# Another order for the first steps of a pooled-attention and maxout kernel: one kv tile summed by TensorE, two others added on GpSimd

## The chip, the cores and the metric

The kernel runs on one core of a Trainium2 chip. A core has five engines that run their own queues of instructions: PE (TensorE, matmuls), DVE (VectorE), ACT (ScalarE), POOL (GpSimd) and SP (SyncE, which here only issues DMAs). The metric is the device time of one execution in microseconds (us); lower is better. Times of the kernel before: 1977.1, 1976.53 and 1977.3 us in three runs, median 1977.1.

## The reference

For each of four batches, 12288 queries of 128 channels attend to 768 keys. The keys are also the values; they come from a 384 x 32 map that is averaged over 4 x 4 windows and multiplied by `w_sr`. The attended rows go through three matrices at once, of which the elementwise maximum is taken, and one output matrix:

```python
kv_pool = kv.reshape(B, H // 4, 4, W // 4, 4, C).mean(axis=(2, 4))
k = v = kv_pool.reshape(B, -1, C) @ w_sr
s = (q @ k.transpose(0, 2, 1)) / np.sqrt(C)
a = np.exp(s - s.max(-1, keepdims=True))
a /= a.sum(-1, keepdims=True) + 1e-09
x = (a @ v).reshape(B * N, C)
h = np.maximum(np.maximum(x @ w1, x @ w2), x @ w3)      # d_ff = 768
out = h @ w_out
```

## The kernel before

The 49152 queries form 96 groups of 512 (four tiles of 128). Values that enter a matmul are split in two float16 parts, high and low, and every product is three matmuls (high by high, high by low, low by high). The maximum over three matrices is computed as `max(0, x(w2-w1), x(w3-w1))`, with `x w1 w_out` added at the end through a matrix `w1o` that is prepared once.

The program is written as a list of short tokens. `START` (lines 169 to 197) is the first part, `STEADY` the repeated middle, `END` the last. `run` (line 1187) executes the tokens in order, and an `InOrder` wrapper (line 98) keeps every engine's instructions in the order in which the tokens issue them, so a token's place sets its place in every queue that it uses. A `!` behind a token changes the engine: for `add`, `fold`, `qc`, `m`, `c`, `l`, `C`, `L` and the weight steps it swaps DVE with POOL or with ACT.

For a group, `S` makes the scores of one tile (six matmuls of 384 columns), `m` the negated row maximum on DVE and the bias `nb` from it, `e` the exponential on ACT, `c` and `l` the float16 parts (`ahl`; ACT and POOL as a rule), after which SP transposes `ahl` into `aT`. `X` multiplies by the values: tile by tile in group 0, later in two halves of a group. `xh`, `xl` split the result; `H` makes six matmuls for one of six column blocks of the hidden layer, `R` and `M` the maximum, `C` and `L` the split `hh`, `hl`; `O` multiplies by `w_out`. `z` is a matmul on constants whose result nobody reads (line 870).

In the first part the keys of batch 0 are made and six weight halves plus two of `w_out` are unpacked. The kv map of a batch is 12 tiles of 512 KB, numbered strip (0 to 2) and row in the window (0 to 3): `kv.s.i` loads one, `add.s.i.n` adds tile n to tile i (128 x 1024 float32), `fold.s.i.n` adds the second half of each window to its first half, and `gat.s.i` sums what is left by matmuls with the identity: eight of 128 columns for a raw tile, four for a folded one. `gd` copies the sums out, `gj` multiplies them by `w_sr`, `gp` and `gb` take the peaks, `gt`, `tops` and `sized` make one power of two out of them, `gh` and `gl` write the keys' two halves; the first `S` needs all of these. `qc` multiplies half a query block by a row of scales, `qp` takes its peak, `qt` turns a group of it by four matmuls with a scaled identity (`sr_e`), `qu` and `qv` split that. The weights go through `wd` (load), `wm` (scale), `ws` (shift), `wt` (column sums on PE), `wl` and `wn` (low bits and sign), `wr` (minus `w1`), `wh` and `wo` (the split). `wl`, `wn` on DVE read two tensors in SBUF.

Of the twelve tiles the kernel before adds `0.1` to `0.0`, `0.3` to `0.2` and their sums on DVE, adds `2.1` and `2.3` to `2.0` there and folds it, and gathers strip 1's four tiles and `2.2` raw. GpSimd has nothing to do there.

Of the kernel before, what the change touches and what calls it, by code (L numbers as in the profile page):

```python
# [21 lines left out]
def kernel(  # L22
# [32 lines left out]
    B, N, C = q.shape  # L55
    _, HH, WW, _ = kv.shape
    R = 4
# [3 lines left out]
    P = 128  # L61
    NKT = NK // P
    NFT = DF // P
    G = 512
# [21 lines left out]
    qp = ctx.enter_context(tc.tile_pool(name="qp", bufs=3))  # L86
# [50 lines left out]
    def spread(out, t, n, start, stop):  # L137
# [21 lines left out]
    wo = [const.tile([P, NFT // 2, 2, C], F16, name=f"wo{h}") for h in range(2)]  # L159
# [7 lines left out]
    HB_ = 5  # L167
    TURNED = 2
    START = (
# [27 lines left out]
    )  # L197
    STEADY = (
# [71 lines left out]
    tops = {}  # L270
# [956 lines left out]
```

## Time and profile before

| | |
|---|---|
| median of three runs | 1977.1 us |
| span of the profiled execution, first to last instruction | 1975.0 us |
| own time of the profiled execution | not listed apart from its span |
| PE busy | 1961.6 us (99%) |
| DVE, ACT, POOL busy | 1449.1, 1494.1, 1306.8 us |
| chain that ended last | PE 97%, DMA 1%, ACT 1% |
| granted TensorE clock | 1.000 over the span (its upper level, 2.4 GHz) |

The median lies 2.1 us above the span. The span holds from the first instruction to the last, so a stretch in which PE has nothing to do lengthens it one for one where PE is busy everywhere behind it. Busy matmuls overlap: a record of 379 ns for 512 columns is issued every 216 ns, so the duration of a row of matmuls is read from one row's start to the next.

### The profile page before, as it was taken

How to read it: one execution, taken by the hardware profiler on the slowest of the kernel's cores; microseconds unless marked ns; L12 is line 12 of the kernel's file. 1: busy time of each engine (PE TensorE's matmuls, PEld its weight loads, DVE VectorE, ACT ScalarE, POOL GpSimd, SP SyncE). 2: the span in 40 equal slices, each digit the busy share in tenths (PEclk: the TensorE clock that was granted, in tenths of full speed). 3: DMA queues.
4: the chain of work that ended last, by engine and by line, in shares of the span. 5: the costliest groups of instructions: out<-in, count | busy, mean ns of one | idle time of the engine just before them, and what ended most of it. 6: DMA issues, size and time to landing. Idle time of an engine off the chain costs nothing.

```text
span 1975.0 us, 29499 instructions
## 1 busy us (share of the span) xinstructions
PE 1961.6 (99%) x9826; PEld 960.4 (49%) x9826; DVE 1449.1 (73%) x2518; ACT 1494.1 (76%) x2628; POOL 1306.8 (66%) x963
## 2 busy tenths in 40 slices
PE   8999999999999999999999999999999999999999
PEld 6444444444444444444444444444444444444444
DVE  7877777777767777777767777777766776766677
ACT  5777777777777777777777777777777777777775
POOL 3576666666667667766676666776676666666663
PEclk9999999999999999999999999999999999999999
DMA  8678777667678778766668777866676666766663
GB/s 272 124 163 164 156 150 144 136 133 145 127 148 167 154 145 164 143 124 142 136 126 169 155 147 157 168 125 128 137 143 138 129 127 125 148 121 125 133 129 80
DMA packets 842696, 283.97 MB, mean 144 GB/s; under 512 B 816048, under 2 KB 817200, under 8 KB 842544
## 3 DMA queue, kind: packets, MB, share of 16 engines
q1 hardware_dynamic: 842256, 281.43, 70.2%
q8 instruction: 77, 1.26, 0.3%
q10 hardware_dynamic: 288, 0.66, 0.1%
q14 instruction: 75, 0.61, 0.1%
HBM read 53.54 MB, written 25.17 MB: 40 GB/s over the span
## 4 chain that ended last, share of the span: by engine, by line
PE 97%; DMA 1%; ACT 1%; POOL 0%; DVE 0%; issue 0%; SPq 0%; POOLq 0%; ACTq 0%
PE ps_h L106 37%; PE ps_o L106 22%; PE ps_x L106 19%; PE ps_s L106 19%; DMA kv_piece<-in_kv_dram 1%; POOL ahl L106 0%; DMA kv_piece<-in_moe_w_out_dram 0%; DMA aT<-ahl 0%; ACT a L106 0%; DVE mx L106 0%; POOL hl L106 0%; DVE w_e L106 0%; ACT ahl L106 0%; ACT w_e L106 0%; ACT h L106 0%
## 5 line engine op out<-in xcount | busy, mean ns | idle before, releaser
L106 POOL TENSOR_TENSOR hl<-h,hh 128x512 f16<-128x512 f32 x469 | 560.8, 1201 | 494.5 <-ACT hh L106 490.6
L106 POOL TENSOR_TENSOR ahl<-a,ahl 128x768 f16<-128x768 f32 x380 | 631.0, 1680 | 104.1 <-ACT ahl L106 79.2
L106 DVE SCALAR_TENSOR_TENSOR h<-ps_h,h 128x512 f32<-128x512 f32 x576 | 396.8, 689 | 365.8 <-PE ps_h L106 209.0
L106 ACT ACTIVATE h<-ps_h 128x512 f32<-128x512 f32 x576 | 343.1, 596 | 274.7 <-PE ps_h L106 264.0
L106 PE MATMUL ps_h<-xh,d_hi 128*128 128x512 f16 x1152 | 436.4, 379 | 0.5 <-ACT h L106 0.2
L106 PE MATMUL ps_h<-xl,d_hi 128*128 128x512 f16 x1152 | 436.4, 379 | 0.0
L106 PE MATMUL ps_h<-xh,d_lo 128*128 128x512 f16 x1152 | 436.4, 379 | 0.0
L106 DVE TENSOR_REDUCE mx<-ps_s 128x1 f32<-128x768 f32 x384 | 365.4, 952 | 51.8 <-PE ps_s L106 51.5
L106 ACT ACTIVATE a<-ps_s,nb,q_sc 128x768 f32<-128x768 f32 x384 | 379.5, 988 | 12.7 <-DVE nb L106 9.0
L106 PE MATMUL ps_s<-k_hi,qT 128*128 128x384 f16 x1536 | 374.7, 326 | 2.1 <-ACT a L106 1.9
L106 PE MATMUL ps_x<-aT,v_hi 128*128 128x512 f16 (+1 forms) x1188 | 366.2, 373 | 0.1
L106 ACT CAST hh<-h 128x512 f16<-128x512 f32 x573 | 333.2, 613 | 42.4 <-DVE h L106 42.4
L106 PEld LDWEIGHTS <-d_hi 128*128 128x128 f16 x2308 | 225.8, 98 | 256.5
L106 PE MATMUL ps_o<-hh,wo 128*128 128x512 f16 x1140 | 339.1, 379 | 0.0
L106 PEld LDWEIGHTS <-qT 128*128 128x128 f16 x2304 | 225.2, 98 | 191.2 <-issue 4.2
L106 ACT CAST ahl<-a 128x768 f16<-128x768 f32 x379 | 309.5, 829 | 7.4 <-DMA aT<-ahl 1.5
L106 PEld LDWEIGHTS <-wo 128*128 128x128 f16 x1710 | 167.3, 98 | 191.7 <-DVE o_planes L106 0.2
L106 PE MATMUL ps_s<-k_lo,qT 128*128 128x384 f16 x768 | 250.3, 326 | 0.0
L106 PE MATMUL ps_x<-aT,v_lo 128*128 128x512 f16 (+1 forms) x594 | 220.1, 373 | 0.0
L106 PE MATMUL ps_o<-hl,wo 128*128 128x512 f16 x570 | 216.0, 379 | 0.0
L106 PEld LDWEIGHTS <-v_hi 128*128 128x128 f16 x1188 | 115.3, 98 | 134.6 <-issue 0.2
L106 PEld LDWEIGHTS <-d_lo 128*128 128x128 f16 x1154 | 112.9, 98 | 122.6 <-issue 3.3
(159 smaller groups left out, 1433.7 us busy)
## 6 DMA issues: line engine op xcount, KB each, us to landing
q_sb<-in_q_dram SPq DMA_DIRECT2D x48, 512.0 KB, 4.4
out_dram<-o_sb SPq DMA_DIRECT2D x95, 256.0 KB, 2.0
kv_piece<-in_kv_dram SPq DMA_DIRECT2D x46, 512.0 KB, 4.5
aT<-ahl SPq DMA_TRANSPOSE x384, 4.0
kv_piece<-in_moe_w_dram SPq DMA_DIRECT2D x6, 384.0 KB, 10.0
o_turned<-o_planes SPq DMA_TRANSPOSE x95, 3.4
qT<-q_hl SPq DMA_TRANSPOSE x94, 3.2
kv_piece<-in_moe_w_out_dram SPq DMA_DIRECT2D x2, 384.0 KB, 4.6
```

What stands on the lines that cost most here:

```text
L106: return lambda **kw: tc.keep_in_program_order(op(**kw))
```

## The change

Only the table `START` changes; the functions, the middle and the end stay, and so does the number of every kind of compute token, with these exceptions. `add.0.2.3` and `gat.1.2` go; `gat.0.3`, `add.1.0.2!` (on GpSimd) and `fold.1.0.2` (on DVE) come. So tile `0.3`, the first loaded, is gathered raw, and strip 1's tiles 0 and 2 are added by GpSimd and folded. The gathers are 48 matmuls in place of 52. The query block is the third load: behind `0.3` on ACT's queue and `1.1` on SP's; strip 2 comes last, its tile 2 in two halves. Eleven `z` stay eleven: one of them stands ahead of the first `S` before, six now. Several weight steps, biases and splits change engine: `qc` twice and `wr` twice from DVE to GpSimd, `wn` twice the other way, `m` twice and `L` three times to GpSimd, `C` three times and `c` twice to DVE, `gd.3` from DVE to ACT. The last token of the new table leaves the same counts of `S`, `X`, `H` and `O` done as before.

```diff
     START = (
-        "qd sr si z ka qc! kv.1.3 gat.1.3 kv.0.2 qc! kv.2.2.0 gat.2.2.0 kv.0.1 qp",
-        "kv.2.2.1 kv.0.0 add.0.0.1 gat.2.2.1 kv.1.1 kv.2.1 add.0.2.3 gat.1.1 kv.2.0 qt add.0.0.2 add.2.0.1 kv.1.0 gat.0.0",
...
+        "z sr z kv.1.1 qd z kv.0.1 qc! si kv.0.0 gat.1.1 qc! kv.0.2 kv.1.0 kv.1.2",
+        "kv.1.3 add.0.0.1 gat.0.3 add.1.0.2! add.0.0.2 ka qp z kv.2.0 gat.0.0 qt qu gp.0 fold.1.0.2 qv",
...
```

GpSimd's queue from its first step on the data, before (`w_s` is a sign, `nb` a bias of `m`, `ahl` the low half of a score tile):

```order
L106 TENSOR_TENSOR w_e_290<-w_e_290,w_s_317 128x384
L106 TENSOR_SCALAR nb_366<-mx_364,q_sc_322 128x1
L106 TENSOR_TENSOR w_e_351<-w_e_351,w_s_375 128x384
L106 TENSOR_SCALAR nb_398<-mx_396,q_sc_322 128x1
L106 TENSOR_TENSOR ahl_409<-a_402,ahl_409 128x768
L106 TENSOR_TENSOR ahl_426<-a_424,ahl_426 128x768
L106 TENSOR_TENSOR ahl_438<-a_429,ahl_438 128x768
```

The same queue now (`kv_piece_189` and `_191` are tiles 1.0 and 1.2, `q_sb_323` the second query block, `ahl_394` the first score tile):

```order
L106 TENSOR_TENSOR kv_piece_189<-kv_piece_189,kv_piece_191 128x1024
L106 TENSOR_TENSOR w_e_284<-w_e_284,w_s_309 128x384
L106 TENSOR_TENSOR w_e_300<-w_e_300,w_s_359 128x384
L106 TENSOR_TENSOR q_sb_323<-q_sb_323,col_row_107 128x512
L106 TENSOR_SCALAR nb_388<-mx_386,q_sc_348 128x1
L106 TENSOR_TENSOR ahl_394<-a_382,ahl_394 128x768
L106 TENSOR_TENSOR q_sb_323<-q_sb_323,col_row_107 128x512
L106 TENSOR_TENSOR ahl_421<-a_416,ahl_421 128x768
L106 TENSOR_TENSOR ahl_445<-a_425,ahl_445 128x768
L106 TENSOR_SCALAR nb_468<-mx_466,q_sc_348 128x1
L106 TENSOR_TENSOR ahl_478<-a_453,ahl_478 128x768
L106 TENSOR_TENSOR w_e_375<-w_e_375,w_e_408 128x384
```

An addition of 1024 columns stands first, and two scalings of queries stand among the low halves.

DVE's queue around the query peak and the scaled identity `sr_e`, before (`kv_piece_197` is tile 0.0, `_178` tile 0.2, `_217` tile 2.0):

```order
L106 TENSOR_REDUCE q_row_190<-q_sb_150 128x1
L106 TENSOR_SCALAR q_row_190<-q_row_190 128x1
L106 TENSOR_SCALAR q_up_192<-q_row_190 128x1
L106 RECIPROCAL q_up_192<-q_up_192 128x1
L106 TENSOR_TENSOR kv_piece_197<-kv_piece_197,kv_piece_188 128x1024
L106 TENSOR_TENSOR kv_piece_178<-kv_piece_178,kv_piece_140 128x1024
L106 TENSOR_SCALAR sr_e_220<-ident_103,q_up_192 128x128
L106 TENSOR_TENSOR kv_piece_197<-kv_piece_197,kv_piece_178 128x1024
L106 TENSOR_TENSOR kv_piece_217<-kv_piece_217,kv_piece_206 128x1024
```

The same stretch now (`kv_piece_175` is tile 0.0, `_189` tile 1.0, `_215` tile 2.0):

```order
L106 TENSOR_TENSOR kv_piece_175<-kv_piece_175,kv_piece_166 128x1024
L106 TENSOR_TENSOR kv_piece_175<-kv_piece_175,kv_piece_187 128x1024
L106 TENSOR_REDUCE q_row_207<-q_sb_162 128x1
L106 TENSOR_SCALAR q_row_207<-q_row_207 128x1
L106 TENSOR_SCALAR q_up_209<-q_row_207 128x1
L106 RECIPROCAL q_up_209<-q_up_209 128x1
L106 TENSOR_SCALAR sr_e_226<-ident_103,q_up_209 128x128
L106 TENSOR_REDUCE pool_max_131<-ps_s_196 128x1
L106 TENSOR_TENSOR kv_piece_189<-kv_piece_189 128x2x256
L106 TENSOR_TENSOR qT_232<-ps_h_225,qT_232 128x4x128
L106 TENSOR_TENSOR kv_piece_215<-kv_piece_215,kv_piece_237 128x1024
```

The strip's additions moved ahead of the query peak, and the fold of strip 1's sum stands between `sr_e` and the addition of strip 2.

## Rows read from the trace of the kernel before

**Rows 1.** The page, busy time of each engine, and the chain's shares.
```profile
PE 1961.6 (99%) x9826; PEld 960.4 (49%) x9826; DVE 1449.1 (73%) x2518; ACT 1494.1 (76%) x2628; POOL 1306.8 (66%) x963
...
PE 97%; DMA 1%; ACT 1%; POOL 0%; DVE 0%; issue 0%; SPq 0%; POOLq 0%; ACTq 0%
```

**Rows 2.** Busy time by stretch: length, engines, granted clock, DMA share, GB/s.
```profile
26.60:60.00 33.40, 29.84 (x203) 16.90 (x203) 31.60 (x63) 29.57 (x55) 19.20 (x17) 1.00 0.76 157
60.00:100.00 40.00, 39.87 (x205) 20.03 (x204) 33.56 (x54) 27.42 (x50) 24.18 (x22) 1.00 0.62 118
```

**Rows 3.** PE in order of time: start, us, instruction, count, idle before.
```profile
14.19 2.05 PE L106 MATMUL ps_s<-ident,kv_piece 128*128 128x128 f32 x16 [0.32 <-DMA kv_piece<-in_kv_dram]
16.07 1.06 PE L106 MATMUL ps_h<-sr_e,q_sb 128*128 128x128 f32 x8
16.97 3.74 PE L106 MATMUL ps_s<-ident,kv_piece 128*128 128x128 f32 x32
...
26.65 0.48 PE L106 MATMUL ps_s<-k_hi,qT 128*128 128x384 f16 x2
...
39.24 2.11 PE L106 MATMUL ps_x<-ones 128*128 128x512 f16 x5
...
55.81 0.38 PE L106 MATMUL ps_x<-aT,v_hi 128*128 128x512 f16 x1
```

**Rows 4.** The chain of waits in order of time: start, us, what.
```profile
89.70 1.29 PE ps_h L106 x6
91.00 1.95 PE ps_s L106 x12
```

**Rows 5.** DVE in order of time, while the kv tiles land.
```profile
7.74 1.22 DVE L106 TENSOR_REDUCE q_row<-q_sb 128x1 f32<-128x1024 f32 x1
...
9.37 0.16 DVE L106 RECIPROCAL q_up<-q_up 128x1 f32<-128x1 f32 x1
12.89 2.36 DVE L106 TENSOR_TENSOR kv_piece<-kv_piece 128x1024 f32<-128x1024 f32 x2 [3.35 <-DMA kv_piece<-in_kv_dram]
```

**Rows 6.** ACT in order of time, ahead of the keys' high half.
```profile
23.71 1.06 ACT L106 ACTIVATE q_abs<-q_sb 128x1024 f16<-128x1024 f32 x1 [0.22 <-DVE q_sb L106]
...
25.21 0.82 ACT L106 ACTIVATE k_hi<-ps_s,k_up 128x256 f16<-128x256 f32 x2
```

**Rows 7.** By tile, whole trace: count, duration ns min/median/max, first and last start.
```profile
L106 POOL TENSOR_TENSOR ahl<-a,ahl x380: 1632/1643/2162, 32.6 to 1941.3; 128x768 f16<-128x768 f32 x190
L106 DVE SCALAR_TENSOR_TENSOR w_e<-kv_piece,w_e x12: 542/549/1221, 27.4 to 63.3; 128x384 int32<-128x384 int32 x12
L106 DVE TENSOR_SCALAR w_e<-w_e x8: 347/354/547, 24.6 to 45.2; 128x384 int32<-128x384 int32 x8
L106 POOL TENSOR_TENSOR w_e<-w_e,w_s x4: 992/1001/1003, 25.8 to 54.3; 128x384 f32<-128x384 f32 x4
L106 DVE SCALAR_TENSOR_TENSOR d_lo<-w_e,d_up,d_hi x4: 612/614/617, 46.4 to 59.1; 128x384 f16<-128x384 f32 x4
L106 DVE SCALAR_TENSOR_TENSOR q_hl<-q_sb,q_up,q_hl x94: 735/743/752, 29.4 to 1912.5; 128x512 f16<-128x512 f32 x94
L106 POOL TENSOR_SCALAR nb<-mx,q_sc x8: 267/561/1078, 29.2 to 99.6; 128x1 f32<-128x1 f32 x8
L106 POOL TENSOR_TENSOR q_sb<-q_sb,col_row x90: 1262/1272/1283, 76.1 to 1847.3; 128x512 f32<-128x512 f32 x90
```

**Rows 8.** POOL and DVE in order of time, at two places where both work.
```profile
50.08 1.64 POOL L106 TENSOR_TENSOR ahl<-a,ahl 128x768 f16<-128x768 f32 x1 [0.90 <-ACT ahl L106]
...
50.91 1.22 DVE L106 SCALAR_TENSOR_TENSOR w_e<-kv_piece,w_e 128x384 int32<-128x384 int32 x1
...
29.15 1.08 POOL L106 TENSOR_SCALAR nb<-mx,q_sc 128x1 f32<-128x1 f32 x1 [2.31 <-DVE mx L106]
...
32.61 1.64 POOL L106 TENSOR_TENSOR ahl<-a,ahl 128x768 f16<-128x768 f32 x1 [0.77 <-ACT ahl L106]
```

**Rows 9.** DMA issues: size, median us from issue to landing.
```profile
aT<-ahl SPq DMA_TRANSPOSE x12, 3.9
```

48 rows, old and new, of the table START are left out of this document.

## The prediction

> **What bounds the kernel.** I read the page's totals and its chain first: PE is busy for 1961.6 us of the 1975.0 us span and carries 97% of the chain [rows 1]. The table by stretch then says where the rest lies: from 60 to 100 us PE has 39.87 of 40.00 us to do, and from 26.6 to 60 only 29.84 of 33.40 [rows 2]. So behind 60 us PE is the bound and any time at which it gets there is carried to the end; what the change can move is the 3.6 us of idle time in that stretch, the fillers `z` (five take 2.11 us at 39.24 [rows 3]) and the start of the scores at 26.65 [rows 3]. In the same stretch DVE is busy for 31.60 of 33.40 us, ACT for 29.57, GpSimd for 19.20 [rows 2]: DVE, not PE, has no room there, and GpSimd is the one with room. In order of time [rows 3, 5] the reader sees what paces the part before: kv tiles land 1.3 us apart (DVE waits for one until 12.89, PE for the next until 14.19), and the last of them is gathered just before the first score.
>
> **A clock for the comparison.** I compare both kernels at one place: the first matmul of `X` of group 1, at 55.81 before [rows 3]. From there PE does not stop. The new order has one more `S` and two more `H` done by then: a `S` is 1.95 / 2 = 0.98 us, a `H` 1.29 us [rows 4], 3.55 us in all. So the new kernel is level with the old one if this `X` starts at 55.81 + 3.55 = 59.36 us; every microsecond earlier is a microsecond gained. That `X` needs the `aT` of group 1's fourth score tile, 3.9 us after its `l` on GpSimd [rows 9]. So the question is when GpSimd ends its eighth `l`.
>
> **Edits ahead of the scores.** The loads keep their number and bytes up to the last kv tile, which lands at the same place in the queue; by moving the queries one place back every tile keeps its 1.3 us grid. Four gathers fewer (48 for 52) save PE 4 x 0.23 = 0.9 us (16 of them, two records each, take 3.74 us from 16.97 [rows 3]), but PE waits for tiles there, so I cost it at nothing; without that cover it would be worth its 0.9. Behind the last load twelve gathers remain in both. Of DVE's additions one goes to GpSimd and a fold comes; DVE waits for tiles there too (3.35 us before 12.89 [rows 5]): nothing. Five of the `z` move ahead of the first score into PE's waits: 5 x 0.21 = 1.05 us leave the later stretch, which counts only as far as PE is short of time there; it is inside the comparison at `X`. On ACT a query peak of 1.06 us stands ahead of the keys' high half before [rows 6] and no longer does: the scores come about 0.5 us sooner, half of that record, since the other half lies beside the size of the keys on DVE. The first bias moves from GpSimd, where it took 1.08 us [rows 8], to DVE; undisturbed it takes 0.267 even on GpSimd [rows 7], which I take for DVE too: 0.8 us. Before, the first `l` starts at 32.61 [rows 8]; so now at 32.61 - 0.5 - 0.8 = 31.3.
>
> **GpSimd's queue from there.** In its new order, from the first to the eighth `l`, stand eight `l` of 1.643, one `qc` of 1.272, four `nb` of 0.561 and four weight subtractions of 1.00 us, for which the sign product of the same shape stands [rows 7]: 13.14 + 1.27 + 2.24 + 4.00 = 20.65 us with hardly a gap. Bare, the eighth `l` ends at 31.3 + 20.65 = 51.95, `X` starts at 51.95 + 3.9 + 0.1 = 55.95, and the change gains 59.36 - 55.95 = 3.4 us.
>
> **What it meets on DVE.** Two places show the two engines in each other's way [rows 8]. At 50.91 DVE starts a weight step that takes 0.549 us as a rule [rows 7] while GpSimd's `ahl` runs from 50.08 to 51.72; it takes 1.22 us and ends 0.41 us behind it. At 29.15 a bias of one column takes GpSimd 1.08 us, against 0.267 at best. Before, GpSimd was idle for 14 of the 33.4 us, so such meetings were few. Now its queue has no gaps, and between the first and the eighth `l` DVE has eight weight steps of 0.549, three `d_lo` of 0.614, one `q_hl` of 0.743 and three shifts or scalings of 0.354 us [rows 7] that read two tensors in SBUF or (the shifts, up to 0.547) were also seen to be held up: 4.39 + 1.84 + 0.74 + 1.06 = 8.0 us. If they never meet, they cost nothing; if the two engines take turns throughout, the eighth `l` is 8.0 us later. I take half, 4.0: GpSimd's neighbour at 50.91 was released 0.13 us before GpSimd's record ended (1.22 - 0.55 = 0.67 after 50.91), pairs of DVE steps queue up once and not twice, and the 94 `q_hl` of the trace never took over 0.752 us although GpSimd works for 66% of the span [rows 1, 7], so a meeting is not certain. A wait of DVE is felt by what is queued behind it: the row maxima, then `nb`, the exponentials on ACT, the next `S` on PE, and the next `c` and `l`, so it does come back to this queue.
>
> The Trainium skill, SBUF — State Buffer, section "Who interferes with whom", says that a DVE instruction with two SBUF inputs, or in a two-port mode, and a GpSimd instruction that reads SBUF exclude each other for the whole instruction. By that rule the full 8.0 us count, the time is that of the second rival, and no release before the end is left. The trace agrees with the exclusion and differs by the 0.13 us.
>
> **The same meeting earlier.** GpSimd's new addition starts when tile 1.2 lands: seventh of the full-size loads in the queue, on the grid the place that landed at 14.19 [rows 3]. No row has 1024 columns on GpSimd; the nearest are 1.00 us for 384 and 1.272 for 512 [rows 7], 2.1 ns a column, so about 2.3 us; bounds are 1.27 (the widest row of that kind seen) and 3.3 (with a DVE step in the way). Its cover is that strip 2's addition on DVE can't start before tile 2.1 lands, three places behind 1.2, at 18.1. But DVE reaches `sr_e` at about 14.5: tile 0.0 lands at 10.3, two additions take 2.36, the peak and its three small steps 1.8 (7.74 to 9.53 [rows 5]). `sr_e` is a scaling inside SBUF, like the shifts; it starts 0.3 us after GpSimd and would wait until 16.4. Behind it on DVE stand the peak of strip 0 and the fold; on PE, `qt` (0.90) and twelve gathers (1.88 + 0.90) [rows 3], so strip 1 is summed at 16.4 + 0.2 + 0.90 + 1.88 + 0.90 = 20.3, where strip 2's addition would let DVE take its peak at 18.1 + 1.2 = 19.3. Price: 1.0 us if the order of starts is this one, 0 if DVE is first. A start difference of 0.3 us on landing times known to about that much is an even chance: I take 0.5.
>
> **Sum.** -3.4 + 4.0 + 0.5 = +1.1 us on the profiled span of 1975.0, 1976.1; the median lies 2.1 us above the span, so 1978.2 us.
>
> **Rivals.**
> 1. GpSimd and DVE miss each other. The 94 undisturbed `q_hl` [rows 7] speak for it, the two meetings [rows 8] against it. The gain is 3.4 us, 1973.7; the most it could be is the idle time plus the five `z`, 3.56 + 1.05 = 4.6, 1972.5.
> 2. Slower: the two engines take turns throughout and GpSimd's queue is the bound of the stretch. The place is the run of `l` in group 0 and 1; the price is 8.0 in place of 4.0 and the whole 1.0 for `sr_e`: -3.4 + 8.0 + 1.0 = +5.6, 1982.7. It decides as soon as more than 3.4 us of the 9.0 come due. For it speaks that the queue has no gaps and that DVE was at 95% in this stretch [rows 2], so no wait is absorbed; against it, that four steps were taken off DVE.
> 3. The change moves next to nothing: the first scores hang on the last kv tile, which lands at the same time, and DVE's fill sets the pace in either order. Then only the 0.5 us at the first score remains, 1976.6. Against it: the DVE work of the stretch does shrink.
>
> **Numbers.** Forecast 0.50, rival 1 0.24, rival 2 0.18, rival 3 0.08. The forecast's own range, with a quarter to three quarters of the 8.0 and 0 to 1.0 for `sr_e`, is 1975.7 to 1980.7. A change of 0.2%, 4.0 us, is about what a measurement of this kernel tells from none. Faster by more than that (under 1973.1): half of rival 1, 0.12. Slower (over 1981.1): most of rival 2 and a small end of the forecast, 0.19. Same 0.69. The range for 8 in 10 reaches from rival 1's lower half to rival 2: 1973.0 to 1982.5.
>
> **What would show it.** In the profile after: GpSimd busy for some 27 us in the 33 us ahead of group 1's `X`, without gaps over 1 us; weight steps on DVE of 1 to 2 us in place of 0.55; `X` of group 1 between 59 and 62. `sr_e` starting near 14.5 and ending near 16.5, and a gap on PE ahead of `qt`. Group 1's `X` at 56 or earlier, with DVE's steps at their usual length, is rival 1; beyond 63 rival 2. It is wrong in another way if PE idles behind that `X`, for then the comparison there does not carry to the end, or if the last kv tile is gathered later than 21.

## The result

| kernel | median us | runs | profiled span |
|---|---|---|---|
| before | 1976.8 | 1976.4 to 1977.3 | 1975.0 |
| after | 1991.7 | 1989.9 to 1993.3 | 1989.2 |

The changed kernel is slower by 14.9 us, a ratio of 1.0076 (95% interval 1.0061 to 1.0090). The forecast was 1978.2 with a range of 1973.0 to 1982.5: the time lies beyond it, on the side of the second rival, and 9.0 us beyond that rival's 1982.7.

### The profile page after: what moved, and what is told of

The parts are those of the page before. It is cut to its first block, busy times and chain, and to the rows that moved or that the text cites. A ratio compares the mean times of both kernels' runs of the same rounds, so it can differ in the third digit from the quotient of the medians.

```text
span 1989.2 us, 29477 instructions
## 1 busy us (share of the span) xinstructions
PE 1964.9 (99%) x9818; PEld 960.7 (48%) x9818; DVE 1458.8 (73%) x2515; ACT 1491.7 (75%) x2622; POOL 1319.8 (66%) x971
## 4 chain that ended last, share of the span: by engine, by line
PE 95%; DVE 3%; DMA 1%; issue 0%; ACT 0%; POOL 0%; SPq 0%; DVEq 0%; POOLq 0%; ACTq 0%
PE ps_h L106 37%; PE ps_o L106 22%; PE ps_x L106 18%; PE ps_s L106 18%; DVE w_e L106 1%; DVE mx L106 1%; DMA kv_piece<-in_kv_dram 0%; DVE h L106 0%; DMA o_turned<-o_planes 0%; DVE ahl L106 0%; DVE wo L106 0%; DVE kv_piece L106 0%; DVE o_planes L106 0%; SPq L106 0%; DVE d_lo L106 0%
```

## The profile after

The totals and the chain's shares, which answer to [rows 1]:

```profile
PE 1964.9 (99%) x9818; PEld 960.7 (48%) x9818; DVE 1458.8 (73%) x2515; ACT 1491.7 (75%) x2622; POOL 1319.8 (66%) x971
...
PE 95%; DVE 3%; DMA 1%; issue 0%; ACT 0%; POOL 0%; SPq 0%; DVEq 0%; POOLq 0%; ACTq 0%
```

PE is busy for 3.3 us more and the span is 14.2 us longer, so 10.9 us are new idle time of PE; DVE, which had no share in the chain, now has 3%. The table by stretch (length, then busy time of PE, PEld, DVE, ACT and POOL, granted clock, DMA share, GB/s) says where; its two middle rows answer to [rows 2].

```profile
14.00:26.60 12.60, 10.12 (x79) 8.47 (x77) 9.56 (x19) 3.46 (x8) 2.52 (x2) 1.00 1.04 398
26.60:60.00 33.40, 24.62 (x177) 16.19 (x178) 31.59 (x58) 24.97 (x46) 23.27 (x20) 0.95 0.70 137
60.00:100.00 40.00, 36.62 (x180) 17.97 (x177) 34.28 (x49) 25.77 (x47) 24.73 (x23) 0.96 0.59 105
100.00:200.00 100.00, 97.97 (x481) 46.95 (x480) 76.64 (x131) 72.45 (x127) 64.03 (x47) 1.00 0.72 153
```

From 14 to 26.6 us PE is idle for 2.5 us instead of 0.2, from 26.6 to 60 for 8.8 instead of 3.6, from 60 to 100 for 3.4 instead of 0.1, and from 100 to 200 for 2.0 instead of nothing. DVE is as busy as before (31.59 of 33.40), yet PE gets 5.2 us less work out of it: DVE's time went into something else. The granted clock is under 1.00 in two places. PE alone, by shorter stretches (length, busy, granted clock, DMA share, GB/s):

```profile
44.00:48.00 4.00, 1.19 (x12) 1.00 0.53 99
48.00:52.00 4.00, 4.00 (x34) 0.57 1.10 139
73.00:76.00 3.00, 0.48 (x3) 0.95 0.70 131
76.00:80.00 4.00, 3.90 (x13) 0.61 0.50 91
```

Both times PE has stood nearly idle for three to four microseconds, and the stretch behind runs mostly at the lower of its two levels (1.2 in place of 2.4 GHz): 4 x 0.43 + 4 x 0.39 = 3.3 us lost, which is also the size of the 3.3 us of added busy time above (the new kernel has eight matmul records fewer, so the two need not be the same). PE in order of time, answering to [rows 3]:

```profile
16.81 1.16 PE L106 MATMUL ps_h<-sr_e,q_sb 128*128 128x128 f32 x8 [1.69 <-DVE sr_e L106]
...
27.50 0.70 PE L106 MATMUL ps_s<-pooled,wsr_sb 128*128 128x256 f32 x2 [1.17 <-ACT k_hi L106]
29.06 0.70 PE L106 MATMUL ps_s<-late,wsr_sb 128*128 128x256 f32 x2 [0.87 <-DVE k_lo L106]
...
30.49 0.49 PE L106 MATMUL ps_s<-k_hi,qT 128*128 128x384 f16 x2
...
47.38 0.33 PE L106 MATMUL ps_o<-w_e,ident 128*128 128x384 bf16 x1 [2.81 <-DVE w_e L106]
...
66.47 0.38 PE L106 MATMUL ps_x<-aT,v_hi 128*128 128x512 f16 x1
...
76.11 0.58 PE L106 MATMUL ps_h<-xh,d_hi 128*128 128x512 f16 x1 [2.62 <-DVE w1o L106]
```

Four things are to be seen. `qt` waits 1.69 us for `sr_e`, as the prediction described. The two projections of the keys, `gj.2` and `gj.3` (27.50, 29.06), wait for the first two strips' halves (`k_hi` on ACT, `k_lo` on DVE); those of the *first* strip still read the PSUM tile that `gj.2` writes. The first score starts at 30.49, not 26.65. `X` of group 1 starts at 66.47, where 59.36 would have been level. And PE waits behind that `X`, too. ACT at the first halves (answers to [rows 6]; the third half waits 2.35 us for `gj.3`), then DVE and GpSimd while the kv tiles land (to [rows 5]):

```profile
26.61 0.84 ACT L106 ACTIVATE k_hi<-ps_s,k_up 128x256 f16<-128x256 f32 x2 [0.26 <-DVE k_up L106]
29.80 0.47 ACT L106 ACTIVATE k_hi<-ps_s,k_up 128x256 f16<-128x256 f32 x1 [2.35 <-PE ps_s L106]
```

```profile
14.83 1.93 DVE L106 TENSOR_SCALAR sr_e<-ident,q_up 128x128 f32<-128x128 f32 x1
...
14.33 2.34 POOL L106 TENSOR_TENSOR kv_piece<-kv_piece 128x1024 f32<-128x1024 f32 x1 [13.04 <-DMA kv_piece<-in_kv_dram]
```

By tile over the whole trace (count, duration ns min/median/max, first and last start), answering to [rows 7]:

```profile
L106 DVE SCALAR_TENSOR_TENSOR w_e<-kv_piece,w_e x14: 545/554/2003, 27.7 to 68.1; 128x384 int32<-128x384 int32 x14
L106 DVE TENSOR_SCALAR w_e<-w_e x8: 343/754/1698, 25.4 to 45.6; 128x384 int32<-128x384 int32 x8
L106 DVE SCALAR_TENSOR_TENSOR d_lo<-w_e,d_up,d_hi x4: 607/636/1101, 50.3 to 62.0; 128x384 f16<-128x384 f32 x4
L106 DVE SCALAR_TENSOR_TENSOR wo<-w_e,u_up,wo x2: 1501/1748/1996, 72.4 to 74.3; 128x384 f16<-128x384 f32 x2
```

The shifts (`TENSOR_SCALAR`) had a median of 354 ns and a maximum of 547; now half of them take over 750. One meeting, GpSimd and DVE side by side, answers to [rows 8]:

```profile
45.48 1.64 POOL L106 TENSOR_TENSOR ahl<-a,ahl 128x768 f16<-128x768 f32 x1
...
45.63 1.70 DVE L106 TENSOR_SCALAR w_e<-w_e 128x384 int32<-128x384 int32 x1
```

The shift starts 0.15 us behind GpSimd's `ahl` and ends 0.21 us behind it: 1.70 us in place of 0.35, and the PE row at 47.38 is the column sum that stood waiting for it. The landing of `aT` did not change (4.0 us in the median of the whole trace, as before; 3.9 in the twelve of [rows 9]).

## The experiments

Times are compared through what each kernel is above the kernel before in the runs made together with it; the interval is that of its ratio to before.

| run | what | us | above before | 95% interval |
|---|---|---|---|---|
| after | | 1991.7 | 14.9 | 1.0061 to 1.0090 |
| h1_loads | new loads, old steps | 1979.43 | 3.1 | 1.0006 to 1.0024 |
| h2_steps | old loads, new steps | 1988.57 | 12.2 | 1.0045 to 1.0078 |
| e1_sr_act | `sr_e` on ACT | 1990.16 | 13.9 | 1.0055 to 1.0085 |
| e2_gj_first | `gj.2`, `gj.3` first | 1989.28 | 13.0 | 1.0050 to 1.0083 |
| e3_both | both | 1987.96 | 11.7 | 1.0043 to 1.0072 |
| e4_engines | nine steps taken off GpSimd and put on DVE | 1995.97 | 19.7 | 1.0083 to 1.0113 |
| e5_fill | PE's two long waits filled | 1989.12 | 12.6 | 1.0050 to 1.0080 |
| e8_prod | e3, `product` first | 1987.53 | 11.2 | 1.0042 to 1.0072 |
| e9_prod_wt | e8, column sums later | 1987.36 | 11.0 | 1.0041 to 1.0071 |
| f1_fills | e3, fills for GpSimd's 8 `ahl` | 1984.92 | 8.3 | 1.0030 to 1.0060 |
| f2_fills_all | f1, fills also for its `ahl` of groups 2, 3 and `hl` of groups 0 to 2 | 1980.34 | 4.0 | 1.0011 to 1.0030 |
| f0_fills, f3_fills_all | before, fills for those of f1's and f2's low halves that GpSimd writes there | 1976.30, 1976.09 | -0.3, -0.3 | 0.9989 to 1.0008, 0.9989 to 1.0007 |
| h3_sr | h1, `sr_e` on ACT | 1978.19 | 1.7 | 0.9999 to 1.0018 |
| h4_qc | h3, two `qc` on GpSimd | 1977.67 | 1.1 | 0.9997 to 1.0016 |
| p1_read, p2_write, p3_write13 | before, with reads or fills on GpSimd | 1983.49, 1978.92, 1982.75 | 7.0, 2.4, 6.2 | 1.0022 to 1.0049, 1.0005 to 1.0025, 1.0020 to 1.0044 |

**Which half of the change.** The start is one list of steps; each half is taken from one of the two kernels.

```diff
 # h1_loads against after
-  ... wd.2.1 gat.2.2.1 wm.1.0 gd.2 gat.2.0 gb gp.2 ws.1.0 gt.2 gt.3 wt.1.0 wm.0.1 wd.3.0 tops gd.3 ...
+  ... gat.2.2.1 gd.2 gat.2.0 gb gp.2 gt.2 gt.3 qd qc! qc! gd.3! tops wd.2.0 wm.2.0! sized ws.2.0 wd.1.0 gj.2 gj.3 ...
 # h2_steps against before
-  ... gat.2.0 gp.1 gt.1 qc! gt.2 gt.3 gd.3! gd.0 gj.0 tops wd.2.0 wm.2.0! sized ws.2.0 wd.1.0 gd.2 gj.2 gj.3 ...
+  ... gat.2.0 gp.1 gt.1 qc! gt.2 gt.3 z z z gd.0 gj.0 gd.1 gj.1 z wd.1.0 wd.0.1 wd.2.1 wm.1.0 gd.2 ws.1.0 wt.1.0 ...
```

> One half of the change alone: the new loads, gathers, additions and folds up to the column sums of the gathered tiles (raw tile 0.3, GpSimd's addition, the early fillers), and from there on the order of steps of the kernel before. Theory (the loss comes from the order of the steps behind the loads: the keys' projections behind the halves, DVE's steps in front of GpSimd's): the time is that of before plus at most the 1.7 us that sr_e waits, 1976.3 to 1978.5. Rival (the loads and GpSimd's addition put the whole start late): 1985 or more.

> The other half alone: the loads, gathers and additions of the kernel before, and from the weights' first step on the new order of steps. Theory (the loss is in the order of steps): 1987 to 1990.5, that is the changed kernel less the 1.5 us that sr_e on ACT brought, and up to 3 us more off if PE's early waits are shorter. Rival (the loads make the loss): 1976 to 1979.

The halves add up (3.1 + 12.2 = 15.3 for 14.9), and their intervals do not overlap: four fifths of the loss lie in the order of the steps behind the loads, as h2's theory had it. The loads cost more than the theory's upper end, 1978.5, by 0.9 us. Under the new loads with the old steps (h1) the two `wo` and all shifts have their usual lengths:

```profile
L106 DVE TENSOR_SCALAR w_e<-w_e x8: 344/352/360, 27.1 to 47.3; 128x384 int32<-128x384 int32 x8
...
L106 DVE SCALAR_TENSOR_TENSOR wo<-w_e,u_up,wo x2: 610/610/611, 62.6 to 67.2; 128x384 f16<-128x384 f32 x2
```

**The two waits ahead of the scores.**

```diff
-            times(st["qup"], ident, st["qr"][g // 2][1])
+            act.mul(out=st["qup"], in_=ident, mul=st["qr"][g // 2][1])      # e1, e3
-    ... wd.1.1 sized gh.1 gh.0 ws.0.1 wl.0.1 z gj.2   qd gl.1 gl.0 gj.3 gh.2 ...
+    ... wd.1.1 z gj.2 gj.3 sized gh.1 gh.0 ws.0.1 wl.0.1   qd gl.1 gl.0 gh.2 ...   # e2, e3
```

> The scaling sr_e of strip 0's peak is written by ACT instead of DVE; GpSimd's addition of strip 1 stays. Port theory (a DVE step inside SBUF waits for a GpSimd step that reads SBUF; ACT does not): sr_e ends near 14.9 us instead of 16.8 and PE's wait of 1.69 us at 16.81 goes. What then reaches the end is bounded by what comes behind: the last kv tile still lands at the same time, so 0 to 1.7 us, about 1 us faster than the changed kernel (1990.7). Rival (the step waits for its input or for its place in DVE's order, not for the port): sr_e ends at 16.8 on ACT too, and the time is 1991.7.

> The last two projections of the keys, gj.2 and gj.3, are issued ahead of the high halves gh.0 and gh.1, which read the PSUM tile that gj.2 writes. PSUM-tile theory (these two projections wait for strip 0's halves, k_hi and k_lo, 1.17 and 0.87 us in the trace): both waits go, the first scores start 2 to 3 us ahead of 30.49 and the time falls by 1.5 to 3 us, to 1988.7 to 1990.2. Rival (the first scores hang on the keys' size and on DVE, whatever the order): first scores at 30.0 to 30.5, time within 1 us of 1991.7.

> sr_e on ACT and gj.2, gj.3 ahead of the halves, together. If both causes are real and in series: the sum of the two gains, 3 to 5 us under 1991.7. If the last kv tile or DVE sets the start of the scores anyway: no more than the larger of the two alone.

In e1 ACT writes `sr_e` beside the same addition of GpSimd in 0.40 us (14.61 to 15.01), and PE's wait of 1.69 us is gone. With both edits, PE before the first scores reads:

```profile
24.14 0.59 PE L106 MATMUL ps_s<-pooled,wsr_sb 128*128 128x256 f32 x2
...
26.53 0.50 PE L106 MATMUL ps_s<-k_hi,qT 128*128 128x384 f16 x2 [0.47 <-DVE k_lo L106]
```

`gj.2` waits for nothing now. The first score stands at 26.53 (29.60 and 28.51 with one edit alone, 30.49 without): both waits were real, and undone together they bring more than the two alone. Some 0.5 us of the 3.96 is not theirs: in this execution the kv tile that GpSimd adds landed at 13.84, in place of 14.33. Group 1's `X` comes at 63.33 in place of 66.47, and the time falls by some 3.2 us. That is the lower end of what was expected of the sum, and each edit alone is within the scatter of the times; the rows carry it. With the scores back at their old start 11.7 us are left, so the loss behind the first score is the larger one.

**Nine steps from GpSimd to DVE.**

```diff
-    ... value.0 ws.2.0 ws.2.1 e qc    ... l c qc l ...   ... m! ...   ... wr.2.0 ... wr.1.0 ...
+    ... value.0 ws.2.0 ws.2.1 e qc!   ... l c qc! l ...  ... m ...    ... wr.2.0! ... wr.1.0! ...
```

> The order is the changed one, but eight steps that it moved are back on the engine of before: two q_sb, five nb and two weight subtractions change between GpSimd and DVE (five nb and both q_sb leave or join GpSimd as in the kernel before, the weight subtractions go back to DVE). Port theory (GpSimd is busy when DVE shifts and scales inside SBUF): GpSimd loses some 7 us in 26.6 to 100 us, DVE's blocked steps of 1.1 to 3.4 us become fewer, the time falls by 2 to 4 us, to 1988 to 1990. Rival (DVE is simply overfull in this stretch): DVE gets more work, so the time rises by 1 to 5 us, to 1993 to 1997.

The rival was right: 19.7 us above before. The edit is not quite what its text says: it moves nine steps, and only six of them (2 `q_sb`, 2 `nb`, 2 subtractions) go back to the engine of before; the other three `nb` stood on GpSimd in the kernel before, too. So it tests how much DVE can take, not the old choice of engines. It left `ahl` on GpSimd, where it meets the shifts, and gave DVE more to do. The waits from 26 to 62 us (in total, times, longest) turned round; GpSimd waits 11.6 us for the high halves, 0.4 in the changed kernel, and ACT waits for the bias behind DVE, 7.5 in place of 1.2:

```profile
POOL ahl L106 <- ACT ahl L106: 11.6, 5, 3.4
...
ACT a L106 <- DVE nb L106: 7.5, 7, 3.1
```

**Where PE stands in its queue.**

```diff
-    ... xh wo.3.0 wo.3.1 product l! S ...
+    ... xh product wo.3.0 wo.3.1 l! S ...                                   # e8, e9
-    ... z c wt.2.1 ka z S wt.2.0 ...  m wt.1.1  e wt.0.0 ... S dsize   qh wt.3.1 ... S wn.2.1
+    ... z c ka z S wt.2.1 wt.2.0 ...  m  e ... S wt.1.1 wt.0.0 dsize   qh ... S wt.3.1 wn.2.1   # e9
```

> The kernel with sr_e on ACT and gj.2, gj.3 ahead of the halves (1987.96), and in addition product issued ahead of the two steps wo.3.0 and wo.3.1, which take 1.75 us each in place of 0.55. Theory (PE's wait of 2.63 us ahead of the second half of a H at 73 us is for product's PSUM tile, which DVE frees only behind these two): the wait goes and the time falls by 2 to 3 us, to 1985 to 1986. Rival (DVE has no room, so the wait only moves to the next H or S): 1987 to 1988.5.

> As the kernel with product moved, and in addition the column sums wt.2.1, wt.1.1, wt.0.0 and wt.3.1 issued behind the S that followed each of them, so that PE does not stand in its queue for a shift on DVE that waits for GpSimd (4.7 us of waits in three places). Theory (PE's place in the queue is the cost): those waits go and the time falls by 2 to 4 us against the kernel without this edit. Rival (the next scores or weights wait for the same DVE steps, and PE only waits elsewhere): within 1 us of it, or slower since the sums come later.

Both rivals were right: 0.5 and 0.2 us, inside the scatter. The named wait goes each time, and another takes its place: with `product` first PE waits for `wo`'s successors (`xl`, 2.0 us in place of 0.2), with the sums later it waits 5.5 us for the scores' PSUM tiles behind ACT's exponentials, in place of 5.9 for the shifts. PE's place by itself was not the cost, which fits the rivals' reason, a DVE without room.

**The clock.**

```diff
+    any_ = ones.bitcast(F16)     # 12 constant matmuls ahead of wt.3.1, 12 ahead of the sixth H
+    for _ in range(12): mm(out=t, lhsT=any_[:, :P], rhs=any_[:, :1].to_broadcast([P, G]), start=True, stop=True)
```

> The changed kernel with 24 constant matmuls more, 12 in each of the two long waits of PE ahead of the stretches in which the granted clock is under 1.00 (48 to 52 us and 76 to 80 us). Clock theory (PE's waits are followed by the lower clock, which costs some 3.3 us in longer matmuls): the clock is 1.00 there and the time falls by 1.5 to 3.5 us, to 1988 to 1990. Rival (where the clock is lower PE waits for DVE anyway, so the longer matmuls hide in the waits): 1991 to 1992.5.

The time falls by some 2.3 us (the intervals overlap). The same stretches of PE:

```profile
44.00:48.00 4.00, 4.00 (x35) 1.00 0.85 147
48.00:52.00 4.00, 3.80 (x48) 1.00 0.54 99
73.00:76.00 3.00, 3.00 (x17) 1.00 0.48 91
76.00:80.00 4.00, 3.75 (x19) 1.00 0.39 73
```

The clock is 1.00 in both places, though it is lower further ahead (0.75 and 0.79 from 26.6 to 34 us) in this profile: its mean from 26.6 to 60 us is 0.95 in both kernels, and group 1's `X` starts at 67.46, no sooner than the 66.47 without fills. So what came back came behind that `X`, where the mean from 60 to 100 us rises from 0.96 to 1.00. The time agrees with the clock theory, but the overlapping intervals don't prove it. Nor is every wait of PE followed by the lower clock: in e3 PE is busy for 0.37 of the 3 us from 70 to 73, and the clock is 1.00 from 73 to 80.

**GpSimd's reads.** First beside the kernel before, where GpSimd is idle between 41 and 62 us: five groups of steps that nothing waits for.

```diff
+    for _ in range(5): pool.tensor_tensor(out=aside, in0=aside, in1=ident, op=ALU.mult)   # p1, at 5 places
+    for _ in range(9): nc.gpsimd.memset(aside, 1.0)                                      # p2 (13 in p3)
```

> The kernel before, with 25 multiplications of a 128x128 scratch tile by a constant tile on GpSimd, in five groups of five that stand where GpSimd is idle between 41 and 62 us; nothing reads the scratch tile. They read two tensors in SBUF. Port theory (DVE's scalings, shifts and steps with two SBUF inputs wait for GpSimd's reads): DVE's steps between 40 and 62 us grow by 2 to 5 us in all, and the time is 1 to 4 us above that of the same kernel with fills in place of the multiplications. Rival (such steps cost only GpSimd's own queue): no more than 0.5 us above the fills.

> The control: the same five places of the kernel before with nine fills of the scratch tile each, about as long on GpSimd, which write SBUF and read nothing there. Port theory: DVE's steps keep the lengths of the kernel before, and the time is within 1 us of 1976.4 but for what GpSimd's own queue comes late. Rival: the same time as with the multiplications.

> The kernel before with 13 fills in each of the five places in place of 9, so that GpSimd is as long at them as at the multiplications (3.2 us a place). Port theory: DVE's steps stay at their usual length, and the time stays 1 to 3 us under the 1983.5 of the multiplications; what it is above the 1978.9 of nine fills is GpSimd's own queue. Rival (the queue alone made the difference): 1983 to 1984.

`d_lo` beside the multiplications, and beside nine fills (with thirteen its median is 610 ns, too):

```profile
L106 DVE SCALAR_TENSOR_TENSOR d_lo<-w_e,d_up,d_hi x4: 807/808/810, 46.9 to 62.0; 128x384 f16<-128x384 f32 x4
```

```profile
L106 DVE SCALAR_TENSOR_TENSOR d_lo<-w_e,d_up,d_hi x4: 606/610/617, 46.1 to 59.5; 128x384 f16<-128x384 f32 x4
```

Beside reads a step of DVE with two inputs in SBUF grows by a third, beside fills of the same place not at all: the mechanism is shown. Its price is not: five multiplications (605 ns each) were longer than nine fills, and with thirteen fills, which are about as long, the kernel is within 0.8 us of the one with multiplications, inside the scatter. The expected 1 to 3 us between these two did not come: p3's 1982.75 lies nearer to its rival. So nearly all of the 7.0 us came from GpSimd's own queue, whose `ahl` were late.

So the price was measured in the new order itself, where the fills take the place of GpSimd's own steps:

```diff
-        (on or pool).tensor_tensor(out=ahl[:, 1], in0=a, in1=ahl[:, 0], op=ALU.subtract)
+        if g < 2 and on is None:        # f1, f0; f2, f3: g < 4, and hl of g < 3 likewise
+            for _ in range(2): nc.gpsimd.memset(ahl[:, 1], 0.0)
+        else: (as before)
```

> The kernel with sr_e on ACT and gj.2, gj.3 first (1987.96), with GpSimd's eight subtractions of the low halves of groups 0 and 1 (ahl) replaced by two fills each of the same tile: the low halves of these two groups are left out. GpSimd stays about as long at it, but reads no SBUF, and the fill does not wait for the high half. Port theory: DVE's weight steps go back from 1.1 to 1.9 us to 0.35 and 0.55, and the time falls by 4 to 7 us, to 1981 to 1984. Rival (the order of DVE's own work is the cost): 1986.5 to 1988.

> The control: the same replacement in the kernel before (those low halves of groups 0 and 1 that GpSimd writes). Port theory: there are few meetings in the old order, so it gains 0 to 2 us, 1974.5 to 1976.5. Rival (fills are shorter or start sooner, and that is what pays): it gains as much as the same replacement in the new order.

> As the kernel with fills for the low halves of groups 0 and 1 in the new order (1984.92), with fills also for GpSimd's low halves ahl of groups 2 and 3 and hl of groups 0 to 2; all these low halves are left out. Port theory: the two wo take 0.55 us each in place of 1.7, PE's wait of 2.7 us at 70 us goes, and the time falls by 2 to 4 us more, to 1981 to 1983. Rival (from 60 us on it is the order of DVE's own work): 1984 to 1985.5.

> The control in the kernel before: the same fills for those of these low halves that GpSimd writes. Port theory: as PE does not wait there from 60 us on, 1975 to 1976.5. Rival (the fills pay by themselves): it gains 2 us or more.

The same place on DVE and GpSimd, two weight steps, in e3 and then in f2:

```profile
37.62 2.46 DVE L106 SCALAR_TENSOR_TENSOR w_e<-kv_piece,w_e 128x384 int32<-128x384 int32 x2
37.98 1.69 POOL L106 TENSOR_TENSOR ahl<-a,ahl 128x768 f16<-128x768 f32 x1 [0.36 <-ACT ahl L106]
```

```profile
36.04 3.10 POOL L780 MEMSET ahl<- 128x768 f16 x4
...
38.48 1.02 DVE L106 SCALAR_TENSOR_TENSOR w_e<-kv_piece,w_e 128x384 int32<-128x384 int32 x2
```

DVE's groups from 14 to 100 us (busy, mean ns), again e3 and then f2:

```profile
L106 DVE SCALAR_TENSOR_TENSOR w_e<-kv_piece,w_e 128x384 int32<-128x384 int32 x14 | 12.3, 887 | 0.1
L106 DVE TENSOR_SCALAR w_e<-w_e 128x384 int32<-128x384 int32 x8 | 6.2, 793 | 0.1
L106 DVE SCALAR_TENSOR_TENSOR wo<-w_e,u_up,wo 128x384 f16<-128x384 f32 x2 | 3.4, 1748 | 0.0
L106 DVE SCALAR_TENSOR_TENSOR d_lo<-w_e,d_up,d_hi 128x384 f16<-128x384 f32 x4 | 3.0, 743 | 0.0
```

```profile
L106 DVE SCALAR_TENSOR_TENSOR w_e<-kv_piece,w_e 128x384 int32<-128x384 int32 x14 | 8.4, 608 | 0.1
L106 DVE TENSOR_SCALAR w_e<-w_e 128x384 int32<-128x384 int32 x8 | 4.3, 559 | 0.1
L106 DVE SCALAR_TENSOR_TENSOR d_lo<-w_e,d_up,d_hi 128x384 f16<-128x384 f32 x4 | 2.4, 610 | 0.0
L106 DVE SCALAR_TENSOR_TENSOR wo<-w_e,u_up,wo 128x384 f16<-128x384 f32 x2 | 1.1, 608 | 0.0
```

The four groups lose 3.9 + 1.9 + 2.3 + 0.6 = 8.7 us. Of DVE's other steps its three casts of `ahl` lose 1.3 us, and one scaling gains 1.4:

```profile
35.21 1.78 DVE L106 TENSOR_SCALAR w_e<-kv_piece 128x384 f32<-128x384 f32 x1
```

This scaling, 0.35 us long in e3, now stands beside GpSimd's `q_sb` and a fill. The kernel falls from 11.7 to 4.0 above before: 7.7 us, where the fills in the old order bring 0.3. The intervals of e3 and f2 do not overlap. f1 alone brought 3.4, less than the 4 to 7 expected, since the two `wo` (1.75 us each there, 0.61 in f2) and PE's 2.7 us behind them were left; the wait is gone in f2.

The fills are a little shorter than `ahl` (1.5 for 1.75 us) and don't wait for the high half, so part of the gain could be GpSimd's shorter queue. The controls don't rule that out: in the old order GpSimd waits up to 2 us ahead of its `ahl`, so a shorter step can gain little there, and only six of the eight `ahl` are its own. Ahead of group 1's `X`, where f1's 3.4 us arise, the eight fills are 1.5 us shorter in all, so up to that much may be the queue. Behind it, where f2 brings 4.3 us more, GpSimd has gaps of 2 to 4 us in f1, so there its queue is not the reason.

**What is left of the loads, and a better version.**

```diff
-    ... gt.3 qd qc! qc! gd.3! tops ...
+    ... gt.3 qd qc qc gd.3! tops ...          # h4, on top of h1 with sr_e on ACT (h3)
```

> The new loads with the old order of steps (1979.43), with sr_e written by ACT in place of DVE, so that it cannot wait behind GpSimd's addition. Theory (most of the 3.1 us that the loads cost is this wait, 1.58 us on PE and 1.65 us on DVE): 1977.5 to 1978.4. Rival (the wait is covered by what comes behind, the last kv tile and the late fold): 1979 to 1979.8.

> The new loads with the old order of steps and sr_e on ACT (1978.19), with the second group's two column scalings of the queries (q_sb, 0.68 us each on DVE, ahead of the last tile's peak) on GpSimd, which is idle there. If DVE's queue sets the first scores: 0.7 to 1.3 us faster, 1976.9 to 1977.5. If GpSimd's two reads hold up DVE's small steps, or the scores hang on the tile's landing: within 0.4 us of 1978.2 or slower.

On this base without the other waits `sr_e` costs 1.3 us of span (1977.7 to 1976.4); ACT writes it in 0.40 us, and PE waits for it no longer. h4 gained 0.6, between the two expectations and inside the scatter. Neither is told from before: no version here beats it.

## Why the prediction was wrong

The forecast span was 1976.1 us and the measured one is 1989.2, 13.1 us more. The place of comparison splits this. With the meetings at 4.0 and `sr_e` at 0.5 the forecast had group 1's `X` at 55.95 + 4.0 + 0.5 = 60.45; it started at 66.47, 6.0 us later. The other 7.1 us arise behind it. The steps in turn:

- **"The scores come about 0.5 us sooner": failed, by 4.3 us.** They came 3.84 later, and the first `l` started at 36.03 in place of 31.8 (31.3 and the 0.5 for `sr_e`): 4.2 of the 6.0 us. `sr_e` and its price (1.0 if the starts are in this order) were right in mechanism and about right in size: 1.69 us of wait, 1.3 us of span in h3. Missed was a wait that the change adds by order alone: `gj.2` writes the PSUM tile that `gh.0` and `gl.0` still read, and now `gj.2` stands behind `gh.0` and `gj.3` behind `gl.0`. The list showed it, and the prediction costed the edits ahead of the scores by engine, not by the tile that they share. Undone together (e3), these two waits are worth 3.2 us.
- **"GpSimd's queue ... with hardly a gap": failed.** With the meetings it had 20.65 + 4.0 = 24.65 us from the first `l` to the end of the eighth. The first starts at 36.03, and the eighth ends at 60.14 + 1.97 = 62.11: 26.1 us. GpSimd stands for 2.09 us until DVE's maximum and for 1.29 until a weight step of DVE:

```profile
36.03 1.64 POOL L106 TENSOR_TENSOR ahl<-a,ahl 128x768 f16<-128x768 f32 x1
...
44.90 0.49 POOL L106 TENSOR_SCALAR nb<-mx,q_sc 128x1 f32<-128x1 f32 x1 [2.09 <-DVE mx L106]
...
48.41 1.00 POOL L106 TENSOR_TENSOR w_e<-w_e 128x384 f32<-128x384 f32 x1 [1.29 <-DVE w_e L106]
...
60.14 1.97 POOL L106 TENSOR_TENSOR ahl<-a,ahl 128x768 f16<-128x768 f32 x1
```

  So up to 48 us DVE sets the pace of this queue, too; behind it GpSimd works without a gap. The lead of 3.4 us was not there: even in f2, without most of the meetings and both early waits, this `X` starts at 60.33, 1.0 us behind the level of 59.36. What led astray was to look for the bound in GpSimd's queue because its work grew, with DVE at 95% in [rows 2].
- **"I take half, 4.0": about right at its place, but the place was too narrow.** Without the reads of the eight `ahl` (f1) `X` comes at 60.55 in place of 63.33, 2.8 us sooner, and the time falls by 3.4. Without those behind (f2) it falls by another 4.3: the sum left out `wo`, 2.3 of DVE's 8.7 us, and what waits for it, because they lie behind the place of comparison. The term for the whole change is up to 7.7 us. The 94 undisturbed `q_hl`, which spoke for the half, lie mostly in the steady part, where the order is another; they said nothing on this stretch.
- **"From there PE does not stop": failed, by 7.1 us, the largest step.** At group 1's `X` the kernel is 66.47 - 59.36 = 7.1 us late, half of the 14.2. The other half arises behind it: 3.4 + 2.0 us of idle time of PE, where before had 0.1, and 1.6 us of lower clock (76 to 80 us). The prediction named this as the way in which it would be wrong otherwise, but gave it neither a price nor a chance. It was true of the old order, and was carried over to the new one unasked.
- **The lower clock: not in the sum at all.** 3.3 us by the rows, half of it on either side of that `X`; some 2 us came back in e5, behind it.
- **A smaller slip:** five `z` take 2.11 us by the row that the prediction names, not 1.05. This enters only the most that rival 1 could gain.
- **Right:** the loads count for little (3.1 us, 1.7 of them left without `sr_e`); tile 1.2 landed on its grid (14.33 for 14.19), and the landing of `aT` did not move; `sr_e` from 14.83 to 16.76, with PE's gap ahead of `qt`; weight steps of 1 to 2 us. Two of its signs of being wrong came true as well: PE idles behind `X`, and the last kv tile is gathered at 22.55, later than 21 (20.52 in e3, so this is mostly the wait for `sr_e`).

The Trainium skill, SBUF — State Buffer, section "Who interferes with whom", says that a DVE step with two SBUF inputs contends with a GpSimd step that reads SBUF, and not with one that only writes there. The runs agree: `d_lo` takes 0.81 us beside multiplications and 0.61 beside fills. The prediction weighed the rule for the whole instruction as rival 2 and gave it 0.18; the time taken from it would still have been 9 us short, for the reasons above.

The account: of the 14.9 us the two waits ahead of the scores make 3.2, GpSimd's reads against DVE's weight steps 7.7 with the waits that follow from them (up to 1.5 of it may be GpSimd's shorter queue), and 4.0 are left in f2. Of these, 1.7 may be the rest of the loads' half, if it adds up here as in h3, where it is not told from nothing. The other 2.3 stay open: in f2 PE still waits for `w_e` (2.2 us), `d_top` (2.0) and `h` (1.7), and its clock is 0.95 from 26.6 to 60 us, but no run took these away one by one.

## What to carry to other kernels

When a list of steps is put in another order, go through it by shared tiles too: a writer moved behind the readers of its PSUM tile waits for them, whatever engine has room. When an engine with no idle time shares something with another one, look for their meetings along the whole *new* order, not up to a place of comparison behind which the old one happened to be tight: more than half of their price lay behind it here. A wait is only the cost if undoing it moves the time: here two kinds of waits of PE could be removed for next to nothing, and others took their place.

## What the runs showed of the hardware

- Beside `ahl` a step of DVE takes nearly the rest of GpSimd's step plus its own: the shift that starts 0.15 us behind a 1.64 us `ahl` takes 1.70 us, so its own 0.35 us begin 0.14 us before GpSimd's record ends; at 50.91 in [rows 8] it is 0.13. Beside a row of multiplications of 605 ns the delay is much less than one of them: `d_lo` takes 0.20 us more (p1).
- Fills hold up DVE's shift of one tensor a little (0.77 us for 0.35, at 41.90 us of f2, beside two fills from 41.72 to 43.35), but not the steps with two inputs behind it (1.01 us for two):

```profile
41.72 1.63 POOL L780 MEMSET ahl<- 128x768 f16 x2
...
41.90 0.77 DVE L106 TENSOR_SCALAR w_e<-w_e 128x384 int32<-128x384 int32 x1
42.59 1.01 DVE L106 SCALAR_TENSOR_TENSOR w_e<-kv_piece,w_e 128x384 int32<-128x384 int32 x2
```

- An addition of 128x1024 in f32 takes GpSimd 2.34 us, beside a waiting DVE step or not (2.35 in e1, where `sr_e` is on ACT), close to the 2.3 that the prediction put between its bounds, against 1.22 on DVE.
